# Attention, a layer of four experts and a squared MLP: the fourth expert taken from seven block products to eight, and the sums of x from GpSimd to VectorE

## The chip, the cores and the metric

One core of one Trainium2 chip runs the whole program. The metric is device time in microseconds (us); before the change it is 771.84 us, the median of three runs (766.21 to 772.74). The profiled execution is a run of its own: 764.1 us.

## The reference

```python
def reference(q, k, v, s, domain_probs, moe_w1, moe_w2, w_in, w_out):
    x = attention(q, k, v, s)               # causal, with a bias from cumsum(max(s, 0)); 2 x 8 heads, 576 x 64
    x = x.transpose(0, 2, 1, 3).reshape(1152, 512)
    p = domain_probs / (domain_probs.sum(-1, keepdims=True) + 1e-9)
    out = 0
    for e in range(4):                      # w1[e] 512 x 1024, w2[e] 1024 x 512
        out += p[:, e:e + 1] * (np.maximum(x @ w1[e], 0) @ w2[e])
    r = np.maximum(out @ w_in, 0)           # w_in 512 x 2048
    return (r * r) @ w_out                  # w_out 2048 x 512
```

All of it is float32. The weights of the last MLP reach the chip as 64-bit numbers (two 32-bit words each) and are turned into float32 there ("decoded").

## The kernel before, in words

**Numbers.** Every operand of the expert layers and of the MLP is split in a high part h = round(x) and a low part l = x - h, and each product is three matmuls (h h, h l, l h). `split` pairs are a cast on ScalarE and a subtraction (`less`, L77) on VectorE or GpSimd.

**The stages.** Experts are counted 0 to 3 here as in the code, E = 4. (1) Attention, with expert 0 for the first 768 tokens filled into its gaps. (2) Expert 0 for the last 384 tokens (L1012), eight steps. (3) Experts 1 to 3 (L1035 to L1066): layer one is done by block products after Strassen and Winograd, seven products of 128 x n x 256 for what plainly takes eight. A group (L962) is one quarter pair q of an expert's weights (12 in all, `NQ`) with one block b of tokens (512 or 640), so there are 24 groups. It has 7 products of 6 matmuls (L934) and, from the group before, the units of layer two (L952). (4) The MLP, as two layers e = E and e = E + 1 of 1024 hidden columns, in 48 steps (L1086): a step is one 128-column slice f of layer one for 384 tokens (`l1_pe`, 12 matmuls of 384 columns, L201; `l1_evac`) and, two steps behind it, the matching part of layer two (`y_quantum`, 9 matmuls of 512 columns, L236). Each layer goes over three thirds of the tokens, eight f each.

**Evacuation.** `l1_evac` of an expert is a relu on ScalarE (L215) and max and subtract on VectorE (L216, reading PSUM). In the MLP it is relu r (L221), g = max(ph, 0) r on VectorE (L223, the last reader of the PSUM tile ph), the cast of g (L226) on ScalarE and h's low part on VectorE (L227, both inputs in SBUF). There are two ph tiles and three h tiles.

**Turning of x.** The output of the experts for 128 tokens is turned by four transposes (L271) into a ph tile and split into xh and xl (`x2_evac`). The nine turnings lie in the last units of the groups (four) and in MLP steps 1 to 5.

**Decoding** (`w_split_double`, L121). One piece is 128 x 512 weights of an MLP half; there are 16 pieces per half, 32 in all. In order: ScalarE L135, GpSimd L137, then VectorE L140, L143, L145, L146, L148, then the cast L154 and GpSimd's subtraction L77. The temporaries dy and dtop exist once; dval has `NV` = 5 buffers. It is a generator with three stages; `advance()` moves each piece in work by one stage, once per step (five times per group). The ten first pieces are put into the last four groups (L1043), six into steps 0 to 4, the 16 of the second half into steps 5 to 20. `slot_free` holds the last stage back until the step at which the slot of its weight is free. A step's y needs one piece of the second weight.

**Order of the work.** A scheduler orders each engine's instructions by a model of their times, with the program's order as priority; SP (which issues the loads) keeps the program's order. Each engine then runs its queue in order.

**Memory.** Weight slots are taken in a ring of nine (`w_slot`), three of the MLP's have their own (`wc_p`). `load_next` keeps three raw pieces ahead (tag raw_w, three buffers, experts and MLP alike); there are 80 loads. `val_tile` takes its tiles from the dval ring.

**Sums.** `x_sums` (L827) makes the sums of blocks of x. For each block b and k2 it adds high and low parts of four quarters on GpSimd (L836, 16 instructions in all), takes four differences on VectorE (L847 to L850) and splits four results; that of b12 is put in place of x's own quarter in xh and xl. `w_pair` (L866) makes the sums and splits of one weight quarter pair (L884 to L912).

Of the kernel before, what the change touches and what calls it, by code (L numbers as in the profile page):

```python
# [8 lines left out]
F32 = mybir.dt.float32  # L9
F32R = mybir.dt.float32r  # L10
# [6 lines left out]
P = 128  # L17
# [16 lines left out]

AK, AQ = slice(0, 2), slice(32, 34)
NA = 6
NV = 5

BLOCKS = ((0, 256), (512, 320))
HIGHEST = 1.4375 * 2.0**-96  # L40
# [3 lines left out]
def fused_kernel(ctx, tc, qk, v, s, dp, w1, w2, wi, wo, out):  # L44
# [40 lines left out]
    def w_load(e, kind, g, half):  # L85
        n = slice(half * 512, (half + 1) * 512)
        if e < E:
            raw = st_pools[0].tile([P, 512], F32, tag=st_pools[2], name="raw_w", bufs=st_pools[1])
            nc.sync.dma_start(out=raw, in_=(w1 if kind == 1 else w2)[e, g, :, n])
        else:  # L90
            raw = st_pools[0].tile([P, 1024], U32, tag="raw_w", name="raw_d", bufs=st_pools[1])
            nc.sync.dma_start(out=raw, in_=(wi if kind == 1 else wo)[e - E, g, half].bitcast(U32))
        wraw[e, kind, g, half] = raw

# [6 lines left out]

    def w_new(e, kind, g):
        if (e, kind, g) not in wt:
            if e == E + 1 and kind == 1 and g:
                wt[e, kind, g] = wc_p.tile([P, 2, 1024], F32R, tag="w", name="w")
            else:
                wt[e, kind, g] = w_slot()
        return wt[e, kind, g]
# [49 lines left out]

    def slot_free(e, kind, g):

        return (e, kind) != (E + 1, 2) or now[0] >= starts[e] - 8 + 2 * g + 2

    PIECES = [(k, g, half) for k in (1, 2) for g in range(4) for half in range(2)]

# [626 lines left out]

    pc_p = ctx.enter_context(tc.tile_pool(name="pc", bufs=1, space=PSUM))
    w8_p = ctx.enter_context(tc.tile_pool(name="w8", bufs=1))
    dbl_p = ctx.enter_context(tc.tile_pool(name="dbl", bufs=1))
    late_p = ctx.enter_context(tc.tile_pool(name="late", bufs=1))
    acc_b = late_p.tile([P, NTILE - NA, DM], F32, name="acc_b")
    for t in range(NA, NTILE):
# [1 line left out]
    st_pools[:] = [late_p, 3, "raw_w"]  # L799
    y_count[0] = 0  # L800
    SKEW = 2
    NQ = (E - 1) * 4


    loads = [(1 + q // 4, k, q % 4, half) for q in range(NQ) for k in (1, 2) for half in range(2)]
    loads += [(e, *piece) for e in (E, E + 1) for piece in PIECES]
    nload = [0]

    def load_next():
# [4 lines left out]
    for _ in range(3):  # L814
# [3 lines left out]
    str_p = sa.enter_context(tc.tile_pool(name="str", bufs=1))  # L818
    h_pools[:] = [str_p, 640, 4]
    tx = {  # L820
        (b, i): str_p.tile([P, 2, 2, n], F32R, name=f"tx{b}{i}") for b, (_, n) in enumerate(BLOCKS) for i in (1, 2, 4)
    }

    def val_tile():
        return dbl_p.tile([P, 512], F32, tag="dval", name="dval", bufs=NV)

    def x_sums(b, k2):  # L827

        t0, n = BLOCKS[b]

        def whole(kk, t):
            x = val_tile()[:, :n]
            nc.gpsimd.tensor_tensor(  # L836
                x, xh[:, kk, t : t + n].bitcast(F32), xl[:, kk, t : t + n].bitcast(F32), op=ALU.add
            )
            return x

        def split(x, hi, lo):
            nc.scalar.copy(hi, x)
            less(nc.vector, lo, x, hi)

        b12, b11 = whole(k2, t0 + n), whole(k2, t0)
        b22, b21 = whole(2 + k2, t0 + n), whole(2 + k2, t0)
        nc.vector.tensor_tensor(b11, b12, b11, op=ALU.subtract)  # L847
        nc.vector.tensor_tensor(b12, b22, b12, op=ALU.subtract)
        nc.vector.tensor_tensor(b22, b22, b11, op=ALU.subtract)
        nc.vector.tensor_tensor(b21, b21, b22, op=ALU.subtract)  # L850
        for i, x in ((1, b11), (2, b22), (4, b21)):
            split(x, tx[b, i][:, 0, k2, :], tx[b, i][:, 1, k2, :])
        split(b12, xh[:, k2, t0 + n : t0 + 2 * n], xl[:, k2, t0 + n : t0 + 2 * n])

    def x_part(b, name, half, k2):
        t0, n = BLOCKS[b]
        x = (xh, xl)[half]
        if name in ("b11", "b21"):
            return x[:, k2 + (2 if name == "b21" else 0), t0 : t0 + n]
        if name in ("b22", "t3"):  # L860
            return x[:, k2 + (2 if name == "b22" else 0), t0 + n : t0 + 2 * n]
        return tx[b, int(name[1])][:, half, k2, :]

    pw = {}
# [1 line left out]
    def w_pair(q):  # L866

        e, g = 1 + q // 4, q % 4

        def quarters(half):  # L870
            return wraw[e, 1, g, half].rearrange("p (k j n) -> p k j n", k=2, j=2)

        def two(x):
            return x.rearrange("p (k n) -> p k n", k=2)

        def raw_parts():
            pw[q] = [w_slot()]
            d = pw[q][0]
            left, right = quarters(0), quarters(1)
            a11, a21 = left[:, :, 0, :], left[:, :, 1, :]  # L880
            a12, a22 = right[:, :, 0, :], right[:, :, 1, :]
            s12, s34 = val_tile(), val_tile()
            s1, s2, s3, s4 = (two(x[:, i : i + 256]) for x in (s12, s34) for i in (0, 256))
            nc.vector.tensor_tensor(s1, a21, a22, op=ALU.add)  # L884
            nc.vector.tensor_tensor(s3, a11, a21, op=ALU.subtract)
            nc.vector.tensor_tensor(s2, s1, a11, op=ALU.subtract)
            nc.vector.tensor_tensor(s4, a12, s2, op=ALU.subtract)
            nc.scalar.copy(two(d[:, 0, 512:768]), a11)
            nc.vector.tensor_tensor(two(d[:, 1, 512:768]), a11, two(d[:, 0, 512:768].bitcast(F32)), op=ALU.subtract)
            raw = wraw[e, 1, g, 1]  # L890
            nc.scalar.copy(d[:, 0, :512], raw)
            less(nc.vector, d[:, 1, :512], raw, d[:, 0, :512])
            for half in range(2):
                wraw.pop((e, 1, g, half))
                load_next()
            pw[q].append((s12, s34))

        def sum_parts(i):
            if i == 0:
                pw[q].insert(1, w_slot())  # L900
            d, x = pw[q][1], pw[q][2][i]
            c = slice(i * 512, i * 512 + 512)
            nc.scalar.copy(d[:, 0, c], x)  # L903
            less(nc.gpsimd, d[:, 1, c], x, d[:, 0, c])

        def second(half):
            raw = wraw.pop((e, 2, g, half))
            t = w_new(e, 2, g)
            n = slice(half * 512, (half + 1) * 512)
            nc.scalar.copy(t[:, 0, n], raw)  # L910
            less(nc.gpsimd, t[:, 1, n], raw, t[:, 0, n])
            load_next()  # L912

        return [
            [raw_parts],
            [lambda: sum_parts(0), lambda: sum_parts(1), lambda: second(0), lambda: second(1)],
        ]

    W_AT = {"a12": (0, 0, 256), "a22": (0, 128, 256), "a11": (0, 512, 128)}
# [89 lines left out]

    c = (768, 384)  # L1010
    prep = {q: w_pair(q) for q in range(NQ)}
    for i in range(NF):  # L1012
        l1_evac(0, c, i, l1_pe(0, c, i))
        if i >= SKEW:
            y_quantum(0, c, i - SKEW)
        if i in (1, 2):
            x_sums(0, i - 1)
        if i >= 4:
            for op in prep[(i - 4) // 2][i % 2]:
                op()  # L1020
    units = [lambda f=f: y_quantum(0, c, f) for f in range(NF - SKEW, NF)]


# [13 lines left out]
    for q in range(2, NQ):  # L1037
        for part in range(2):
            side[2 * q - 3 + part] += prep[q][part]
    side[0] += [lambda: x_sums(1, 0)]  # L1040
    side[1] = [lambda: x_sums(1, 1)] + side[1]
    last = len(groups) - 1
    for g in range(4):  # L1043
        for half in range(2):
            side[last - 3 + g].append(lambda g=g, half=half: decode(E, 1, g, half))
    for half in range(2):
        side[last].append(lambda half=half: decode(E, 2, 0, half))
    x2q = []
    for i, (q, b) in enumerate(groups):
        todo = units  # L1050
        n_units, n_side = len(todo), len(side[i])
# [2 lines left out]
        def do_next(k):  # L1054
# [5 lines left out]
            while done[1] < n_side * (k + 1) // 5:  # L1060
                side[i][done[1]]()
                done[1] += 1
            advance()

        units = group(q, b, do_next)
    now[0] = -1  # L1066


    for t, unit in enumerate(units):
        if t < 4:  # L1070
            x2_evac(t, x2_pe(t))
        unit()
    sa.close()
    mlp_p = ctx.enter_context(tc.tile_pool(name="mlp", bufs=1))
    h_pools[:] = [mlp_p, 384, 3]
    wc_p = ctx.enter_context(tc.tile_pool(name="wc", bufs=3))
    y_slots[:] = [yb_p] * 5 + [pc_p]
    thirds = [(0, 384), (384, 384), (768, 384)]
    seq = [(e, c, f) for e in (E, E + 1) for c in thirds for f in range(NF)]
    starts = {E: 0, E + 1: 24}  # L1080
    wsched = {}
    for n, (g, half) in enumerate((g, half) for g in range(1, 4) for half in range(2)):
        wsched.setdefault(n * 5 // 6, []).append((E, 2, g, half))
    for n, piece in enumerate(PIECES):
        wsched.setdefault(5 + n, []).append((E + 1, *piece))
    for i in range(len(seq) + SKEW):  # L1086
        now[0] = i
        advance()
        if i < len(seq):
            e, c, f = seq[i]  # L1090
            l1_evac(e, c, f, l1_pe(e, c, f))
        if 1 <= i < 6:
            x2_evac(3 + i, x2_pe(3 + i))
        if SKEW <= i < len(seq) - HOLD + SKEW:
            y_quantum(*seq[i - SKEW])
        for w in wsched.get(i, []):
            decode(*w)

    e, c, _ = seq[-1]
    tiles = range(c[0] // P, (c[0] + c[1]) // P)  # L1100
# [54 lines left out]
```

## Time and profile before

| | |
|---|---|
| median of three runs | 771.84 us |
| the three runs | 771.84, 772.74, 766.21 us |
| the profiled execution | 764.1 us |
| its span, first to last instruction | 762.3 us |
| mean granted clock of TensorE | 0.991 |

In the rows below times are in us unless they say ns. PE is TensorE, PEld its weight loads, DVE VectorE, ACT ScalarE, POOL GpSimd, SP the engine that issues the DMAs. Matmuls overlap in the pipeline, so the sum of their records is more than the time they take; paces are therefore read from start to start. A bracket at the end of a row of the timeline is the idle time of the engine before it and what ended it.

### The profile page before, as it was taken

What the parts mean: (1) busy time and instruction counts of PE and PEld (TensorE: products, weight loads), DVE (VectorE), ACT (ScalarE), POOL (GpSimd) and SP (SyncE); (2) the same over time, 40 slices, a digit from 0 to 9 for tenths busy, and PEclk for the clock granted to TensorE, in tenths of its full rate; (3) what the DMA queues carried; (4) which work ended last, traced back from release to release, by engine and by line L of the source; (5) the groups of instructions that cost most, each with busy time, mean ns of one, the idle gap of its engine ahead of it and who ended that gap; (6) DMA issues with size and microseconds to landing.
All of it is one profiled execution on the core that took longest, in us unless ns stands there. A gap on an engine that the chain in (4) does not pass through costs nothing.

```text
span 762.3 us, 11177 instructions
## 1 busy us (share of the span) xinstructions
PE 714.1 (94%) x3974; PEld 609.4 (80%) x3974; DVE 472.1 (62%) x1061; ACT 322.3 (42%) x756; POOL 225.5 (30%) x256
## 2 busy tenths in 40 slices
PE   5989999989988999999999999999877999968998
PEld 3567778767977898989989999898766899857996
DVE  7886666553389446454464546777767786777332
ACT  4787666553244243342343424334433333333221
POOL 6654433331277022130221304221222212222000
PEclk9999999999999999999999999999999999999999
DMA  6752232200122012010120103211222221220111
GB/s 185 217 163 70 76 96 63 57 24 1 42 74 66 28 39 73 28 56 28 47 65 28 56 29 103 77 56 55 84 77 68 78 78 61 83 84 0 42 42 41
DMA packets 28823, 50.37 MB, mean 66 GB/s; under 512 B 3424, under 2 KB 12144, under 8 KB 28768
## 3 DMA queue, kind: packets, MB, share of 16 engines
q1 hardware_dynamic: 28768, 49.67, 21.3%
q8 instruction: 31, 0.51, 0.3%
q14 instruction: 24, 0.20, 0.1%
HBM read 45.28 MB, written 2.54 MB: 63 GB/s over the span
## 4 chain that ended last, share of the span: by engine, by line
PE 79%; DVE 10%; issue 3%; DMA 3%; ACT 3%; POOL 2%; SPq 0%; DVEq 0%; POOLq 0%; ACTq 0%
PE y L952 19%; PE ph L201 15%; PE y L236 14%; PE ph L934 12%; PE o L602 5%; PE pc L934 5%; PE pt L555 4%; PE s L464 2%; DVE h L227 2%; PE s L465 2%; POOL w L77 1%; DMA raw_w<-in_w 1%; PE s L449 1%; DVE dtop L143 1%; ACT dy L135 1%
## 5 line engine op out<-in xcount | busy, mean ns | idle before, releaser
L201 PE MATMUL ph<-xh,w 128*128 128x384 f32 (+1 forms) x640 | 168.2, 330 | 21.3 <-DVE g L223 17.8
L952 PE MATMUL y<-w,h 128*128 128x512 f32 x648 | 170.1, 393 | 0.0
L236 PE MATMUL y<-w,h 128*128 128x512 f32 x648 | 165.5, 396 | 4.3 <-ACT w L154 4.3
L236 PEld LDWEIGHTS y<-w,h 128*128 128x128 f32 x648 | 119.6, 189 | 29.1 <-ACT w L154 8.5
L201 PEld LDWEIGHTS ph<-xh,w 128*128 128x128 f32 x640 | 115.6, 192 | 32.5 <-DVE g L223 22.7
L77 POOL TENSOR_TENSOR w<-dval,w 128x512 fp32r<-128x512 f32 x56 | 76.8, 1375 | 188.5 <-ACT w L903 143.1
L952 PEld LDWEIGHTS y<-w,h 128*128 128x128 f32 x648 | 114.9, 188 | 16.2
L201 PE MATMUL ph<-xl,w 128*128 128x384 f32 (+1 forms) x320 | 104.3, 327 | 0.0
L934 PE MATMUL ph<-xh,w 128*128 128x256 f32 (+1 forms) x288 | 69.2, 297 | 3.4 <-DVE h L983 1.9
L221 ACT ACTIVATE r<-ph 128x384 f32<-128x384 f32 x48 | 23.6, 491 | 108.6 <-PE ph L201 103.7
L201 PEld LDWEIGHTS ph<-xl,w 128*128 128x128 f32 x320 | 61.5, 192 | 3.5 <-issue 1.5
L532 POOL TENSOR_SCALAR p<-p,stat 128x128 f32<-128x128 f32 (+8 forms) x80 | 45.7, 585 | 52.7 <-DVE stat L529 35.4
L227 DVE TENSOR_TENSOR h<-g,h 128x384 fp32r<-128x384 f32 x48 | 40.2, 838 | 31.6 <-ACT h L226 31.6
L137 POOL TENSOR_SCALAR dy<-dy 128x512 f32<-128x512 f32 x32 | 20.3, 635 | 130.0 <-ACT dy L135 130.0
L982 ACT ACTIVATE h<-c 128x256 fp32r<-128x256 f32 (+1 forms) x72 | 31.9, 444 | 57.4 <-DVE c L979 57.4
L934 PEld LDWEIGHTS ph<-xh,w 128*128 128x128 f32 x288 | 50.1, 188 | 7.2 <-DVE h L983 2.3
L516 ACT ACTIVATE p<-p,stat 128x128 f32<-128x128 f32 (+9 forms) x80 | 46.6, 583 | 21.0 <-DVE stat L502 19.3
L983 DVE SCALAR_TENSOR_TENSOR h<-c,h 128x256 fp32r<-128x256 f32 (+1 forms) x72 | 39.7, 551 | 20.1 <-ACT h L982 19.9
L223 DVE SCALAR_TENSOR_TENSOR g<-ph,r 128x384 f32<-128x384 f32 x48 | 26.7, 556 | 36.4 <-ACT r L221 35.8
L934 PE MATMUL ph<-tx,w 128*128 128x256 f32 (+1 forms) x288 | 45.9, 296 | 0.3 <-ACT p L973 0.3
L934 PEld LDWEIGHTS ph<-tx,w 128*128 128x128 f32 x288 | 42.6, 189 | 3.3 <-ACT p L973 0.5
L502 DVE CUSTOM_DVE_ANT_0 p<-s,mask 128x448 f32<-128x448 f32 (+7 forms) x64 | 30.5, 477 | 22.7 <-PE pt L555 10.9
(120 smaller groups left out, 1137.3 us busy)
## 6 DMA issues: line engine op xcount, KB each, us to landing
raw_w<-in_w SPq DMA_DIRECT2D x64, 256.0 KB
raw_d<-in_wi SPq DMA_DIRECT2D x16, 512.0 KB
raw_d<-in_wo SPq DMA_DIRECT2D x16, 512.0 KB
raw<-in_qk SPq DMA_DIRECT2D x40, 144.0 KB
v<-in_v SPq DMA_DIRECT2D x8, 256.0 KB
out<-acc_a SPq DMA_DIRECT2D x6, 256.0 KB
tl<-th SPq DMA_DIRECT2D x8, 144.0 KB
raw_p<-in_qk SPq DMA_DIRECT2D x4, 256.0 KB
```

Source lines behind the costliest of these rows:

```text
L77: eng.tensor_tensor(out_, a, b.bitcast(F32), op=ALU.subtract)
L201: nc.tensor.matmul(ps[:, :n], lhsT=w1_ap(e, wh, kk, f), rhs=x[:, kk, t0 : t0 + n], start=(i == 0), stop=(i == 3 * KD - 1),)
L227: nc.vector.tensor_tensor(t[:, 1, :n], g[:, :n], t[:, 0, :n].bitcast(F32), op=ALU.subtract)
L236: mm = nc.tensor.matmul(ps, lhsT=h[:, hh, o : o + P], rhs=w2_ap(e, wh, f), start=(f == 0 and i == 0), stop=(f == NF - 1 and i == 2),)
L502: nc.vector.tensor_tensor_reduce(t.p[: t.n, a:z], ps[: t.n, : z - a], t.bias[:, a:z], scale=-0.125, scalar=init, op0=ALU.add, op1=ALU.min, ...
L516: nc.scalar.activation(t.p[: t.n, : t.w], t.p[: t.n, : t.w], AF.Exp, bias=t.nmax, scale=-1.0, accum_out=t.st[: t.n, 4 + t.c : 5 + t.c],)
L532: nc.gpsimd.tensor_scalar(t.p[: t.n, : t.w], t.p[: t.n, : t.w], t.st[: t.n, 6 + t.c : 7 + t.c], 1.0, op0=ALU.mult, op1=ALU.mult)
L602: nc.tensor.matmul(u.o[i * D : (i + 1) * D, qs - u.q0 : u.nq], lhsT=vv[:kn, j, i * D : (i + 1) * D], rhs=rhs, start=(j == 0), stop=(j == j ...
L934: nc.tensor.matmul(ps[:, :n], lhsT=pw[q][s][:, wh, c : c + P], rhs=x_part(b, xn, xx, k2), start=(first and m == 0), stop=(m == 5), skip_gr ...
L952: nc.tensor.matmul(ps, lhsT=hs[j][:, hh, o : o + P], rhs=wt[e, 2, g][:, wh, j * DM : (j + 1) * DM], start=(g % 2 == 0 and i == 0 and j == ...
L982: nc.scalar.activation(hs[j][:, 0, cols], ps[:, :n], AF.Relu)
L983: nc.vector.scalar_tensor_tensor(hs[j][:, 1, cols], ps[:, :n], 0.0, hs[j][:, 0, cols].bitcast(F32), op0=ALU.max, op1=ALU.subtract)
```

## The change

Expert 3 goes from the groups to the front of the plain steps: `NQ` is 8 (experts 1 and 2), there are 16 groups, and `seq` has 72 steps, 24 each for e = 3, E and E + 1. The splits of expert 3's weights lie in the last four groups and in steps 0 to 3. The 16 decoded pieces of E lie at steps 3 to 21, those of E + 1 at steps 23 to 43. The turnings of x follow each third of expert 3 (one per step, from the step after its last y). `NV` is 6, dbl_p opens after the groups, raw_d has three buffers of its own there, the value tiles of the sums are four of their own ("val"), and other weights use wc_p. The sums of `x_sums` are on VectorE, and b12 has a tile of its own (expert 3 needs x as it is). `w_pair` does the same instructions in smaller parts (sums, raw_hi, raw_lo, sum_hi, sum_lo, second_hi, second_lo). The preparations of the first groups are placed by the list `first`.

```diff
-NV = 5
+NV = 6
...
-            raw = st_pools[0].tile([P, 1024], U32, tag="raw_w", name="raw_d", bufs=st_pools[1])
+            raw = dbl_p.tile([P, 1024], U32, tag="raw_d", name="raw_d", bufs=3)
...
-            if e == E + 1 and kind == 1 and g:
+            if g and (e, kind) in ((E, 1), (E + 1, 2)):
...
-        return (e, kind) != (E + 1, 2) or now[0] >= starts[e] - 8 + 2 * g + 2
+        return kind == 1 or now[0] >= starts[e] - 8 + 2 * g + 2
...
-    NQ = (E - 1) * 4
+    PLAIN = E - 1
+    NQ = (PLAIN - 1) * 4
...
-    loads += [(e, *piece) for e in (E, E + 1) for piece in PIECES]
+    loads += [(e, *piece) for e in range(PLAIN, E + 2) for piece in PIECES]
...
-        return dbl_p.tile([P, 512], F32, tag="dval", name="dval", bufs=NV)
+        return str_p.tile([P, 512], F32, tag="val", name="val", bufs=4)
...
-            nc.gpsimd.tensor_tensor(
+            nc.vector.tensor_tensor(
                 x, xh[:, kk, t : t + n].bitcast(F32), xl[:, kk, t : t + n].bitcast(F32), op=ALU.add
             )
...
-        for i, x in ((1, b11), (2, b22), (4, b21)):
+        for i, x in ((1, b11), (3, b12), (2, b22), (4, b21)):
             split(x, tx[b, i][:, 0, k2, :], tx[b, i][:, 1, k2, :])
-        split(b12, xh[:, k2, t0 + n : t0 + 2 * n], xl[:, k2, t0 + n : t0 + 2 * n])
...
+    first = [[lambda: x_sums(0, 0)], [lambda: x_sums(0, 1)], [], []]
+    first += [prep[0][0], prep[0][1], prep[1][0], prep[1][1][:2]]
...
-        if i in (1, 2):
-            x_sums(0, i - 1)
-        if i >= 4:
-            for op in prep[(i - 4) // 2][i % 2]:
-                op()
+        for op in first[i]:
+            op()
...
-    side[0] += [lambda: x_sums(1, 0)]
+    side[0] = prep[1][1][2:] + [lambda: x_sums(1, 0)]
...
-            side[last - 3 + g].append(lambda g=g, half=half: decode(E, 1, g, half))
-    for half in range(2):
-        side[last].append(lambda half=half: decode(E, 2, 0, half))
+            side[last - 3 + g].append(lambda g=g, half=half: split(PLAIN, 1, g, half))
+    for g in range(2):
+        for half in range(2):
+            side[last].append(lambda g=g, half=half: split(PLAIN, 2, g, half))
...
-    for t, unit in enumerate(units):
-        if t < 4:
-            x2_evac(t, x2_pe(t))
+    for unit in units:
         unit()
     sa.close()
...
+    dbl_p = ctx.enter_context(tc.tile_pool(name="dbl", bufs=1))
...
-    seq = [(e, c, f) for e in (E, E + 1) for c in thirds for f in range(NF)]
-    starts = {E: 0, E + 1: 24}
-    wsched = {}
-    for n, (g, half) in enumerate((g, half) for g in range(1, 4) for half in range(2)):
-        wsched.setdefault(n * 5 // 6, []).append((E, 2, g, half))
-    for n, piece in enumerate(PIECES):
-        wsched.setdefault(5 + n, []).append((E + 1, *piece))
+    seq = [(e, c, f) for e in range(PLAIN, E + 2) for c in thirds for f in range(NF)]
+    starts = {e: 24 * (e - PLAIN) for e in range(PLAIN, E + 2)}
+    wsched = {n: [(PLAIN, 2, 2 + n // 2, n % 2)] for n in range(4)}
+    for e in (E, E + 1):
+        for n, piece in enumerate(PIECES):
+            at = starts[e - 1] + (3 + n * 5 // 4 if e == E else n * 22 // 16 - 1)
+            wsched.setdefault(at, []).append((e, *piece))
+    x2q = []
...
-        if 1 <= i < 6:
-            x2_evac(3 + i, x2_pe(3 + i))
-        if SKEW <= i < len(seq) - HOLD + SKEW:
-            y_quantum(*seq[i - SKEW])
+        if x2q and x2q[0][0] <= i:
+            t = x2q.pop(0)[1]
+            x2_evac(t, x2_pe(t))
+        if i >= SKEW:
+            e, c, f = seq[i - SKEW]
+            if i - SKEW < len(seq) - HOLD:
+                y_quantum(e, c, f)
+            if e == E - 1 and f == NF - 1:
+                x2q += [(i + 1 + n, t) for n, t in enumerate(range(c[0] // P, (c[0] + c[1]) // P))]
         for w in wsched.get(i, []):
-            decode(*w)
+            split(*w) if w[0] < E else decode(*w)
```

## Rows read from the trace of the kernel before

**Rows 1.** The page: busy time of each engine, share of the span, instructions.

```profile
PE 714.1 (94%) x3974; PEld 609.4 (80%) x3974; DVE 472.1 (62%) x1061; ACT 322.3 (42%) x756; POOL 225.5 (30%) x256
```

**Rows 2.** Busy time by stretch: length, then each engine's, clock, DMA share, GB/s.

```profile
200.00:235.00 35.00, 32.66 (x161) 29.64 (x160) 28.09 (x45) 14.42 (x34) 24.43 (x22) 0.95 0.23 76
235.00:262.00 27.00, 23.35 (x143) 20.34 (x143) 17.73 (x36) 9.81 (x25) 8.41 (x7) 1.00 0.16 49
...
379.80:426.90 47.10, 47.10 (x277) 42.60 (x277) 24.52 (x50) 17.28 (x40) 10.85 (x8) 1.00 0.15 45
...
527.60:587.20 59.60, 47.41 (x233) 40.43 (x232) 43.04 (x70) 22.63 (x44) 16.78 (x18) 0.97 0.24 77
587.20:650.00 62.80, 62.80 (x318) 57.02 (x317) 48.58 (x82) 24.59 (x48) 15.21 (x17) 1.00 0.22 69
650.00:699.00 49.00, 39.11 (x188) 32.57 (x187) 36.21 (x56) 16.45 (x33) 14.67 (x16) 1.00 0.19 63
```

**Rows 3.** The chain of waits in order of time: start, length, what.

```profile
385.64 2.73 PE y L952 x12
...
432.72 2.73 PE y L952 x12
...
527.85 2.10 PE ph L201 x12
...
603.14 2.04 PE y L236 x9
...
648.53 2.04 PE y L236 x9
...
663.70 1.42 DVE h L227
...
690.17 1.42 DVE h L227
...
752.38 6.13 PE y L236 x27
```

**Rows 4.** Timeline of PE in the last stage: start, length, instructions, idle before.

```profile
522.64 0.60 PE L271 MATMUL ph<-ident,acc_a 128*128 128x128 f32 x4
...
533.50 0.45 PE L201 MATMUL ph<-xh,w 128*128 128x384 f32 x1 [1.05 <-DVE g L223]
...
669.92 0.98 PE L236 MATMUL y<-w,h 128*128 128x512 f32 x3 [0.45 <-ACT w L154]
672.37 0.45 PE L201 MATMUL ph<-xh,w 128*128 128x384 f32 x1 [1.47 <-DVE g L223]
```

**Rows 5.** Timeline of VectorE: ends of decoded pieces, and one piece whole.

```profile
490.88 0.68 DVE L148 SCALAR_TENSOR_TENSOR dval<-dtop,dy 128x512 f32<-128x512 f32 x1
...
507.45 0.69 DVE L148 SCALAR_TENSOR_TENSOR dval<-dtop,dy 128x512 f32<-128x512 f32 x1
...
641.38 0.68 DVE L148 SCALAR_TENSOR_TENSOR dval<-dtop,dy 128x512 f32<-128x512 f32 x1
...
648.21 0.69 DVE L148 SCALAR_TENSOR_TENSOR dval<-dtop,dy 128x512 f32<-128x512 f32 x1
...
672.23 0.42 DVE L140 TENSOR_SCALAR dtop<-dy 128x512 uint32<-128x512 uint32 x1
...
674.60 0.69 DVE L148 SCALAR_TENSOR_TENSOR dval<-dtop,dy 128x512 f32<-128x512 f32 x1
```

**Rows 6.** Groups over the span: busy us, mean ns of one, idle before and releasers.

```profile
L201 PE MATMUL ph<-xh,w 128*128 128x384 f32 x448 | 126.4, 345 | 20.1 <-DVE g L223 17.8 <-DVE h L216 2.3
...
L77 POOL TENSOR_TENSOR w<-dval,w 128x512 fp32r<-128x512 f32 x56 | 76.8, 1375 | 188.5 <-ACT w L903 143.1 <-ACT w L154 42.0 <-PE y L952 3.3
...
L227 DVE TENSOR_TENSOR h<-g,h 128x384 fp32r<-128x384 f32 x48 | 40.2, 838 | 31.6 <-ACT h L226 31.6
```

**Rows 7.** The same groups, VectorE alone, from 200 to 262 us.

```profile
L216 DVE SCALAR_TENSOR_TENSOR h<-ph,h 128x384 fp32r<-128x384 f32 x8 | 4.4, 546 | 0.0
...
L847 DVE TENSOR_TENSOR dval<-dval 128x320 f32<-128x320 f32 x2 | 1.0, 478 | 0.0
```

More of the change, by code (lines that the diff above doesn't have):

```diff
@@ L793, in fused_kernel @@
     w8_p = ctx.enter_context(tc.tile_pool(name="w8", bufs=1))
-    dbl_p = ctx.enter_context(tc.tile_pool(name="dbl", bufs=1))
     late_p = ctx.enter_context(tc.tile_pool(name="late", bufs=1))
@@ L820, in fused_kernel @@
     tx = {
-        (b, i): str_p.tile([P, 2, 2, n], F32R, name=f"tx{b}{i}") for b, (_, n) in enumerate(BLOCKS) for i in (1, 2, 4)
+        (b, i): str_p.tile([P, 2, 2, n], F32R, name=f"tx{b}{i}") for b, (_, n) in enumerate(BLOCKS) for i in (1, 2, 3, 4)
     }
     def val_tile():
-        return dbl_p.tile([P, 512], F32, tag="dval", name="dval", bufs=NV)
+        return str_p.tile([P, 512], F32, tag="val", name="val", bufs=4)
     def x_sums(b, k2):
@@ L859, in x_part @@
             return x[:, k2 + (2 if name == "b21" else 0), t0 : t0 + n]
-        if name in ("b22", "t3"):
-            return x[:, k2 + (2 if name == "b22" else 0), t0 + n : t0 + 2 * n]
+        if name == "b22":
+            return x[:, k2 + 2, t0 + n : t0 + 2 * n]
         return tx[b, int(name[1])][:, half, k2, :]
@@ L874, in two, with parts, sums @@
             return x.rearrange("p (k n) -> p k n", k=2)
-        def raw_parts():
-            pw[q] = [w_slot()]
-            d = pw[q][0]
+        def parts():
             left, right = quarters(0), quarters(1)
[L880 to L883, printed above, removed]
+            return left[:, :, 0, :], left[:, :, 1, :], right[:, :, 0, :], right[:, :, 1, :]
+        def sums():
+            a11, a21, a12, a22 = parts()
+            x = [val_tile(), val_tile()]
+            s1, s2, s3, s4 = (two(v[:, i : i + 256]) for v in x for i in (0, 256))
             nc.vector.tensor_tensor(s1, a21, a22, op=ALU.add)
@@ L887, in raw_parts, with raw_hi, raw_lo @@
             nc.vector.tensor_tensor(s4, a12, s2, op=ALU.subtract)
[L888 to L892, printed above, removed]
+            pw[q] = [w_slot(), w_slot(), x]
+        def raw_hi():
+            d = pw[q][0]
+            nc.scalar.copy(two(d[:, 0, 512:768]), parts()[0])
+            nc.scalar.copy(d[:, 0, :512], wraw[e, 1, g, 1])
+        def raw_lo():
+            d = pw[q][0]
+            nc.vector.tensor_tensor(
+                two(d[:, 1, 512:768]), parts()[0], two(d[:, 0, 512:768].bitcast(F32)), op=ALU.subtract
+            )
+            less(nc.vector, d[:, 1, :512], wraw[e, 1, g, 1], d[:, 0, :512])
             for half in range(2):
@@ L895, in raw_parts, with sum_hi, sum_lo, second_hi @@
                 load_next()
[L896 to L901, printed above, removed]
-            c = slice(i * 512, i * 512 + 512)
[L903 to L908, printed above, removed]
+        def sum_hi():
+            for i, x in enumerate(pw[q][2]):
+                nc.scalar.copy(pw[q][1][:, 0, i * 512 : i * 512 + 512], x)
+        def sum_lo(i):
+            c = slice(i * 512, i * 512 + 512)
+            less(nc.gpsimd, pw[q][1][:, 1, c], pw[q][2][i], pw[q][1][:, 0, c])
+        def second_hi(half):
+            nc.scalar.copy(w_new(e, 2, g)[:, 0, half * 512 : half * 512 + 512], wraw[e, 2, g, half])
+        def second_lo(half):
             n = slice(half * 512, (half + 1) * 512)
-            nc.scalar.copy(t[:, 0, n], raw)
-            less(nc.gpsimd, t[:, 1, n], raw, t[:, 0, n])
+            t = wt[e, 2, g]
+            less(nc.gpsimd, t[:, 1, n], wraw.pop((e, 2, g, half)), t[:, 0, n])
             load_next()
         return [
-            [raw_parts],
-            [lambda: sum_parts(0), lambda: sum_parts(1), lambda: second(0), lambda: second(1)],
+            [sums, raw_hi, raw_lo],
+            [
+                sum_hi,
+                lambda: (sum_lo(0), second_hi(0)),
+                lambda: (sum_lo(1), second_hi(1)),
+                lambda: (second_lo(0), second_lo(1)),
+            ],
         ]
@@ L1039, in fused_kernel, with split @@
             side[2 * q - 3 + part] += prep[q][part]
-    side[0] += [lambda: x_sums(1, 0)]
+    side[0] = prep[1][1][2:] + [lambda: x_sums(1, 0)]
     side[1] = [lambda: x_sums(1, 1)] + side[1]
     last = len(groups) - 1
+    def split(*piece):
+        w_split(*piece)
+        load_next()
     for g in range(4):
         for half in range(2):
-            side[last - 3 + g].append(lambda g=g, half=half: decode(E, 1, g, half))
-    for half in range(2):
-        side[last].append(lambda half=half: decode(E, 2, 0, half))
-    x2q = []
+            side[last - 3 + g].append(lambda g=g, half=half: split(PLAIN, 1, g, half))
+    for g in range(2):
+        for half in range(2):
+            side[last].append(lambda g=g, half=half: split(PLAIN, 2, g, half))
     for i, (q, b) in enumerate(groups):
@@ L1062, in do_next @@
                 done[1] += 1
-            advance()
         units = group(q, b, do_next)
-    now[0] = -1
-    for t, unit in enumerate(units):
-        if t < 4:
-            x2_evac(t, x2_pe(t))
+    for unit in units:
         unit()
```

## The prediction

> **What bounds the kernel now.** I read the page's engine line first: PE is busy 94% of the span, which says little, because it is a mean over stages [rows 1]. The busy time by stretch comes next. The reader is to see that in four product groups (379.8 to 426.9) and in 587.2 to 650 PE has no idle time at all, while 527.6 to 587.2 leaves 59.60 - 47.41 = 12.2 us idle, 650 to 699 leaves 9.9 us, and the start of the expert stage 2.3 and 3.7 us [rows 2]. The chain of waits gives the pace. Two places four groups apart lie 432.72 - 385.64 = 47.08 us from each other, so a group is 11.77 us. A step of a plain layer (12 matmuls of layer one, 9 of layer two) takes (648.53 - 603.14) / 11 = 4.126 us where PE never waits. In 663.70 to 690.17 the chain runs through VectorE's L227 instead, four steps in 26.47 us, 6.62 us each [rows 3]. PE's own timeline says what a 6.62 us step waits for: 0.45 us on ScalarE's cast of the second weight (L154), which the decoding has only just delivered, and 1.47 us on VectorE's L223, which frees the PSUM tile [rows 4]. So in both stretches the weights of the last MLP arrive one piece per step, exactly as they are consumed. The whole last stage lasts 752.38 + 6.13 - 527.85 = 230.7 us [rows 3]; 48 steps at 4.126 are 198.1 us, and five turnings of x (L271) at 0.60 us or less are 3.0 us [rows 4]. **29.6 us of it are waits for decoded weights** and what follows from them.
>
> Why are they late? One piece is about 3.06 us of VectorE (L140 at 672.23 to the end of L148 at 675.29), behind a step on ScalarE and one on GpSimd, and its buffer dy is single, so pieces follow each other. L148 comes every (507.45 - 490.88) / 2 = 8.28 us among the product groups and every 6.83 us beside the squared layer at full PE speed [rows 5]. Thirty-two pieces begin in the last four groups, and the last is wanted about 200 us later. At 6.8 to 8.3 us each that is not enough.
>
> **The change part by part.**
>
> *Expert three in eight products.* Eight groups go, 2 x 47.08 = 94.2 us. Twenty-four plain steps come, 24 x 4.126 = 99.0 us. Cost: +4.9 us of PE. I take the step at 4.126 although its evacuation differs: L216 instead of r, g, cast and L227. That is less for VectorE (0.546 us in one instruction against L227 with 0.84 us and L223 besides) and hidden under PE [rows 6, 7]. The sums of this expert's weights, its sum splits and the additions L979 go too. They lay under fully busy PE, with VectorE at 24.5 of 47.1 us [rows 2], so I cost them at nothing.
>
> *Decoding beside expert three.* The first piece starts at about step 4 of 72, where before it lay among the groups, and the last is due at step 57. Sixteen pieces are spread at one per 1.25 steps (5.2 us) beside expert three, sixteen at one per 1.375 steps beside the first half of the MLP. VectorE's load beside expert three is 0.546 + 3.06 / 1.25 = 3.0 us of a 4.126 us step (without its evacuation of y, three instructions in eight steps). Beside the MLP it was busy 48.58 of 62.80 us, which are 15.2 steps, with nine pieces; at one per 1.375 steps it would have eleven, 48.58 + 2 x 3.06 = 54.7 [rows 2, 5, 7]. It fits, but not loosely. What pace will the chain of one dy keep? The bounds are 5.2 us (the schedule) and 8.28 us (among groups). I take 6.0 us beside expert three, since there a step has one short VectorE instruction where the groups have several that wait for PE, and 6.83 us beside the MLP, the row of the same work. From step 4 (447 us by the sum below) E's pieces are then done at 447 + 96 = 543, and its last is due at step 33 (568). The last MLP half is done at 543 + 109 = 652 and due at step 57 (667). Both are in time, so the 29.6 us go. What is late next is the turning of x: nine, each between a layer one product and its y, where before gaps of 1.05 us on L223 stood behind it [rows 4]. Now each has nine y matmuls beside it, so I take half of 1.05 us for nine, and 1 us for the change of stage: **6 us remain**, bounds 0 and 12.
>
> *New waits.* The ScalarE cast of a second weight waits until its slot is free (program step 18 + 2g, 42 + 2g). Behind it on ScalarE stand the relu of the next step and the next piece's L135. The slot's last reader is layer one of step 17 + 2g (41 + 2g), which has run by then, so it costs nothing in order; if it slips, six value buffers (five before) cover it, and a missed one costs one 4.1 us step. On SP the eighty loads keep their order. The raw tiles of the MLP now lie in memory that opens when the groups end, so their first load goes out around step 1; the first weight is due at step 24, 83 us later. The splits of expert three's weights in the last four groups take no more than the preparation that stood there. All that is zero; if the cover of the last group fails, a single late split costs about 1 us.
>
> *Sums of x.* Sixteen instructions leave GpSimd and come to VectorE. The nearest VectorE row of kind and width (L847, 320 columns; half of them are narrower) is 0.478 us, so some 16 x 0.48 = 7.7 us are added in a stretch where VectorE is busy 28.1 of 35 and 17.7 of 27 us [rows 2, 7]. Of PE's 2.3 + 3.7 = 6.0 us idle there 2.3 wait for VectorE's L216 [rows 2, 6]. Bounds: -6 us, all of it, and +4 us, half of the added work, if L216 falls further behind. I take -2, the gap on L216, because GpSimd's slower turn no longer stands ahead of the subtractions. The product of b12 now has its own tile; that is the same number of splits, so nothing.
>
> The Trainium skill has a rule that speaks against this move ("SBUF — State Buffer", section "SBUF: two separate sides"): a VectorE operation with two SBUF inputs and a GpSimd operation reading SBUF exclude each other for the whole instruction. The trace agrees in kind: L227, both inputs in SBUF, takes 0.84 us in the mean and 1.42 us in the chain, L216, with one input in PSUM, 0.546 [rows 3, 6, 7]. By the rule each of the sixteen sums could stand behind one GpSimd subtraction (1.375 us [rows 6]), an estimate of 22 us against 16.2 us of VectorE's idle time there, which would put about +6 us in place of -2; the same rule also frees the others from sixteen GpSimd instructions, and I keep the -2.
>
> **Sum.** The last stage starts at 527.85 - 94.2 - 4 x 0.60 (four turnings lay there) - 2 = 429.3. Then 72 x 4.126 = 297.1, nine turnings 5.4, waits 6, and from PE's end to the span's end 762.3 - 758.5 = 3.8: span 741.6 us. The profiled execution is 764.1 for a span of 762.3, so 743.4 in its terms, 20.7 us less. It lies 7.7 us under the median of the three runs (771.84, 772.74, 766.21); carried over whole, that gives 751.1, and by the lowest run 745.5. I say **748 us**.
>
> **Rivals.**
> 1. *The decoding stays late (slower).* The pace remains 8.28 us, as in the groups, because VectorE's queue sets decoding steps behind evacuations that wait for PE. Then 447 + 32 x 8.28 = 712, 45 us after step 57: 748 + 45 = 793 us. It eats the whole gain from (667 + 21 - 447) / 32 = 7.5 us per piece on. For it: the groups' rows and the single dy. Against: 6.83 us beside the heavier layer [rows 5]. Chance 0.10.
> 2. *Weights are in time, but decoding ahead of the evacuation in VectorE's queue makes PE wait for its PSUM tile.* At 0.8 us for each of 32 pieces that is 26 us, 774: no change. For it: the 1.05 us gap on L223. Against: 587.2 to 650, with nine pieces and no idle PE [rows 2, 4, 5]. Chance 0.13.
> 3. *No waits at all remain*, and the start loses none: 748 - 6 - 4 = 738 us. Chance 0.12.
>
> The forecast has 0.65. Its own range is 739 to 760 (residual waits 0 to 12, start -6 to +4, run to run from 745.5 to 751.1). The 8-in-10 range is 736 to 768, which leaves out rival 1 and most of rival 2. About 1% is what a measurement tells here, 764.1 to 779.6: faster 0.77 (forecast and rival 3), same 0.13, slower 0.10.
>
> **What would show it.** Right: PE idle under 8 us from the end of the groups to the end; steps at about 4.13 us across 72; no y matmul waiting for L154; L148 every 5 to 6.5 us beside expert three; sixteen groups still 11.77 us each. Wrong: 6.6 us steps again, in the MLP's first or second half (rival 1); gaps on L216 or L223 after decoding instructions (rival 2); a start of the expert stage with more than 6 us idle (the sums of x).

## The result and the profile after

The changed kernel takes 735.8 us in the median of four runs (734.63 to 741.11), beside it the kernel before 769.44 us (766.21 to 772.74): a ratio of 0.958, 95% interval 0.951 to 0.964. The forecast was 748 us, with 739 to 760 as its own range and 736 to 768 as the wide one: the result lies at the lower edge of the wide range and under the narrow one. Thirteen later runs of the kernel before have 766.7 us in the median, so the gain is nearer 31 us than 34.

The profiled execution is the slowest of the four, 741.11 us with a span of 739.3. Attention, whose code is the same, lasted until 207.3 us in it (granted clock 0.93 up to there), and until 200.2 us in the profile before (0.98) and 200.8 us in a later run of nearly the same kernel; these 7 us are not the change's. Places are therefore compared from the start of the expert stage, its first matmul of 384 columns. From there to the end of the span it takes 562.1 us before and 532.0 us now: 30.1 us less.

The busy time by stretch of the changed kernel (columns as in rows 2) answers to [rows 2]:

```profile
207.46:242.00 34.54, 34.54 (x184) 31.77 (x184) 27.14 (x60) 15.58 (x35) 11.52 (x8) 1.00 0.26 84
242.00:269.00 27.00, 25.13 (x149) 21.63 (x148) 20.51 (x42) 10.41 (x26) 5.56 (x4) 1.00 0.11 39
...
431.30:540.00 108.70, 108.12 (x559) 98.19 (x558) 73.32 (x117) 33.10 (x63) 24.97 (x27) 1.00 0.25 79
540.00:640.00 100.00, 100.00 (x516) 91.42 (x515) 72.09 (x125) 39.11 (x77) 24.96 (x26) 1.00 0.21 69
640.00:735.56 95.56, 95.56 (x484) 86.66 (x482) 48.40 (x82) 28.49 (x56) 10.96 (x11) 1.00 0.10 36
```

The reader is to see the first two columns: PE's busy time is the whole stretch nearly everywhere. The plain steps have 0.58 us of idle PE in 304 us, where 12.2 + 9.9 us stood in two stretches before. The start of the expert stage keeps 1.9 of 6.0 us.

The chain of waits in order of time answers to [rows 3]:

```profile
280.65 2.75 PE y L961 x12
...
327.78 2.75 PE y L961 x12
...
576.75 2.04 PE y L236 x9
...
630.40 2.04 PE y L236 x9
...
729.44 6.13 PE y L236 x27
```

Four groups take 47.13 us, as before. Thirteen steps take 630.40 - 576.75 = 53.65 us, 4.127 each, with a decoding of the last MLP half beside them. No step of 6.6 us is left. The last wait of PE in the start of the stage and its only one after that, 0.58 us at the seam of the groups and the steps, are in its timeline:

```profile
254.53 0.98 PE L943 MATMUL pc<-tx,w 128*128 128x256 f32 x6 [1.17 <-DVE c L988]
...
438.08 1.66 PE L236 MATMUL y<-w,h 128*128 128x512 f32 x6 [0.58 <-ACT h L215]
```

The decoding itself did not become faster. VectorE's timeline, the first and the last piece of each half, answers to [rows 5]:

```profile
445.21 0.69 DVE L148 SCALAR_TENSOR_TENSOR dval<-dtop,dy 128x512 f32<-128x512 f32 x1
...
553.28 0.69 DVE L148 SCALAR_TENSOR_TENSOR dval<-dtop,dy 128x512 f32<-128x512 f32 x1
...
561.58 0.69 DVE L148 SCALAR_TENSOR_TENSOR dval<-dtop,dy 128x512 f32<-128x512 f32 x1
...
674.71 0.69 DVE L148 SCALAR_TENSOR_TENSOR dval<-dtop,dy 128x512 f32<-128x512 f32 x1
```

Fifteen intervals make 7.20 us a piece for the MLP's first half and 7.54 us for its second: slower than the forecast's 6.0 and 6.83. It is in time all the same, because it begins earlier. The first and the last piece in VectorE's timeline of the kernel before:

```profile
471.21 1.75 DVE L148 SCALAR_TENSOR_TENSOR dval<-dtop,dy 128x512 f32<-128x512 f32 x1
...
701.42 0.69 DVE L148 SCALAR_TENSOR_TENSOR dval<-dtop,dy 128x512 f32<-128x512 f32 x1
```

Over all 31 intervals the pace is 7.43 us before and 7.40 us now. Counted from the start of the expert stage, the first piece moves from 271.0 to 237.9 us and the last from 501.2 to 467.4 us, while the MLP begins where it did (327.5 and 325.5 us). So it is the earlier start that the change buys, not a faster decoding beside a lighter evacuation.

### The profile page after: what moved, and what is told of

Its sections match the earlier page's. It is cut to its first block, busy times and chain, and to the rows that moved or that the text cites. A ratio compares the mean times of both kernels' runs of the same rounds, so it can differ in the third digit from the quotient of the medians.

```text
span 739.3 us, 10968 instructions
## 1 busy us (share of the span) xinstructions
PE 711.9 (96%) x3926; PEld 614.3 (83%) x3926; DVE 448.7 (61%) x1028; ACT 309.4 (42%) x716; POOL 188.4 (25%) x224
## 4 chain that ended last, share of the span: by engine, by line
PE 89%; DVE 5%; DMA 3%; POOL 1%; issue 1%; ACT 1%; SPq 0%; POOLq 0%; DVEq 0%; ACTq 0%
PE ph L201 27%; PE y L236 25%; PE y L961 13%; PE ph L943 8%; PE o L602 5%; PE pt L555 3%; PE pc L943 3%; PE s L464 2%; DMA raw_w<-in_w 2%; PE s L465 2%; POOL w L77 1%; DVE w L77 1%; DMA s<-in_s 1%; PE ph L271 1%; DVE tx L77 0%
## 5 line engine op out<-in xcount | busy, mean ns | idle before, releaser
L201 PE MATMUL ph<-xh,w 128*128 128x384 f32 (+1 forms) x832 | 218.2, 328 | 1.6 <-DVE h L216 1.6
L201 PEld LDWEIGHTS ph<-xh,w 128*128 128x128 f32 x832 | 149.5, 190 | 8.1 <-DVE h L216 2.4
L201 PE MATMUL ph<-xl,w 128*128 128x384 f32 (+1 forms) x416 | 135.7, 327 | 0.0
L201 PEld LDWEIGHTS ph<-xl,w 128*128 128x128 f32 x416 | 78.9, 190 | 5.0 <-issue 1.5
L137 POOL TENSOR_SCALAR dy<-dy 128x512 f32<-128x512 f32 x32 | 20.3, 634 | 198.4 <-ACT dy L135 132.9
L223 DVE SCALAR_TENSOR_TENSOR g<-ph,r 128x384 f32<-128x384 f32 x48 | 26.7, 556 | 50.1 <-ACT r L221 50.1
L77 POOL TENSOR_TENSOR w<-val,w 128x512 fp32r<-128x512 f32 x16 | 23.3, 1461 | 130.0 <-ACT w L903 89.2
L215 ACT ACTIVATE h<-ph 128x384 fp32r<-128x384 f32 (+1 forms) x56 | 24.5, 444 | 69.2 <-PE ph L201 59.1
L77 POOL TENSOR_TENSOR w<-dval,w 128x512 fp32r<-128x512 f32 x32 | 41.7, 1302 | 37.1 <-ACT w L154 37.1
L216 DVE SCALAR_TENSOR_TENSOR h<-ph,h 128x384 fp32r<-128x384 f32 (+1 forms) x56 | 27.5, 495 | 38.8 <-ACT h L215 38.7
L943 PE MATMUL ph<-tx,w 128*128 128x320 f32 (+1 forms) x288 | 45.8, 296 | 0.7 <-ACT u L982 0.7
L555 PE MATMUL pt<-ident,p 128*128 128x128 f32 (+3 forms) x232 | 40.6, 289 | 4.0 <-POOL p L532 3.7
```

Source lines behind the costliest of these rows:

```text
L77: eng.tensor_tensor(out_, a, b.bitcast(F32), op=ALU.subtract)
L201: nc.tensor.matmul(ps[:, :n], lhsT=w1_ap(e, wh, kk, f), rhs=x[:, kk, t0 : t0 + n], start=(i == 0), stop=(i == 3 * KD - 1),)
L216: nc.vector.scalar_tensor_tensor(t[:, 1, :n], ps[:, :n], 0.0, t[:, 0, :n].bitcast(F32), op0=ALU.max, op1=ALU.subtract)
L555: nc.tensor.transpose(tp_ap(t, j), t.p[: t.n, kt[j] : kt[j + 1]], ident[: t.n, : t.n])
L943: nc.tensor.matmul(ps[:, :n], lhsT=pw[q][s][:, wh, c : c + P], rhs=x_part(b, xn, xx, k2), start=(first and m == 0), stop=(m == 5), skip_gr ...
```

## The experiments

The theory was that the gain is time for a decoding whose pace one dy buffer sets, and that the sums of x on VectorE give a little at the start. Against it stood: that queue order sets the pace, that the plain steps' lighter evacuation is the gain, and that the placement of the preparation cleared the start.

**One part alone: two buffers of dy in the kernel before.**

```diff
-NV = 5
+NV = 4
-        y = tmp(F32, "dy")
+        y = tmp(F32, "dy", 2)
```

> The kernel before with two buffers of dy (dval 4 instead of 5, for the room), nothing else. If the single dy sets the pace of the decoding: L148 comes every 6 us or less among the product groups instead of 8.28, the waits of 29.6 us in the last stage fall by 15 to 25 us, ratio 0.97 to 0.98. If the order of VectorE's and ScalarE's queues (decoding steps behind evacuations) sets it: the pace stays at 7 to 8 us, ratio 0.995 to 1.01.

Measured: 750.32 us (749.49 to 751.17), ratio 0.977, interval 0.973 to 0.981. The second and the last piece in VectorE's timeline of this run:

```profile
482.42 0.68 DVE L148 SCALAR_TENSOR_TENSOR dval<-dtop,dy 128x512 f32<-128x512 f32 x1
...
647.14 0.69 DVE L148 SCALAR_TENSOR_TENSOR dval<-dtop,dy 128x512 f32<-128x512 f32 x1
```

Thirty intervals are 164.7 us, 5.49 us each, where the kernel before has 7.43 us. The single dy set the pace, and about half of the gain (766.8 us, the median of seven runs of the kernel before beside it, to 750.3) is to be had by that alone. But the kernel does not reach 736, although its PE work is the smaller: VectorE is now the limit. Its slices on the page (busy tenths, 40 slices) stand at 9 from the 27th to the 34th:

```profile
DVE  6785666454178656455464455899999999823232
```

The chain of waits of this run goes through the decoding itself, of which this is one piece:

```profile
602.38 1.59 DVE dtop L143
```

**One part alone: the sums of x on VectorE in the kernel before.**

```diff
-            nc.gpsimd.tensor_tensor(
+            nc.vector.tensor_tensor(
                 x, xh[:, kk, t : t + n].bitcast(F32), ...
```

> The kernel before with the sixteen sums of x on VectorE, nothing else. If GpSimd's sums make the PE gaps at the start of the expert stage (6.0 us): 3 to 6 us less, ratio 0.992 to 0.996, and PE idle there under 3 us. If the new placement and the smaller parts of the preparation are what took them away: ratio 1.00, the gaps stay.

Measured: 760.26 us, ratio 0.990, interval 0.986 to 0.994, a little faster than either theory said. The gaps at the start became smaller and others took their place: PE is idle 4.1 us there, not under 3. The largest gap left in PE's timeline:

```profile
244.53 0.39 PE L934 MATMUL ph<-xh,w 128*128 128x256 f32 x1 [2.00 <-DVE c L979]
```

The first y L952 x12 after 270 us is the same place in the groups in every run. By the chain of the kernel before it comes 79.1 us after the start of the expert stage (200.2):

```profile
279.29 2.72 PE y L952 x12
```

In this run it comes 75.8 us after (202.9):

```profile
278.75 2.72 PE y L952 x12
```

So the start is 3.3 us shorter, but not by the sums alone: the granted clock was 0.95 over 35 us of it before [rows 2], a mean of full level (2.4 GHz) and half, and 1.00 here: an estimated 1.7 us (35 x 0.05). A further 2.7 us lie in the last stage, whose waiting steps take 6.1 us here; why this edit shortens them stays open. The next run asks the same question more cleanly.

**One part undone: the sums back on GpSimd in the changed kernel.**

```diff
-            nc.vector.tensor_tensor(
+            nc.gpsimd.tensor_tensor(
                 x, xh[:, kk, t : t + n].bitcast(F32), ...
```

> The changed kernel with the sixteen sums of x back on GpSimd, nothing else. If the engine of the sums makes the gaps at the start of the expert stage: 3 to 6 us more, 739 to 742. If their placement does: 736, no change.

Measured: 739.44 us (738.66 to 741.69), 3.6 us over the changed kernel's median. The gap on L216 is back in PE's timeline:

```profile
238.18 0.39 PE L943 MATMUL ph<-xh,w 128*128 128x256 f32 x1 [1.39 <-DVE h L216]
```

The same place comes 76.8 us after the stage's start, 73.4 us in the changed kernel and 74.1 to 74.3 us in two later runs with the same start. So the engine is worth some 3 us. That the other 2.3 us (79.1 to 76.8) come from the placement in smaller parts is not shown. The first run leaves sums and placement as they were (only the ring that the sums share is one buffer shorter), and there the place comes 76.6 us after the start (202.3):

```profile
278.94 2.72 PE y L952 x12
```

One profile each cannot tell 2.3 us of placement from a difference of that size without it.

**A later decoding, by the schedule's numbers.**

```diff
-            at = starts[e - 1] + (3 + n * 5 // 4 if e == E else n * 22 // 16 - 1)
+            at = starts[e - 1] + (11 + n * 13 // 16 if e == E else n * 22 // 16 - 1)
```

> The changed kernel with the 16 pieces of E put at steps 11 to 23 instead of 3 to 21, nothing else. If the gain is the earlier start of the decoding, at a pace of 7.2 to 7.5 us a piece that stays as it is: all ends some 8 steps (33 us) later, steps of 6.6 us with waits on L154 come back, 20 to 30 us more, 756 to 766. If the place of the decoding beside expert three's lighter evacuation is the gain and the start is not: under 5 us more.

Measured: 736.33 us (735.51 to 737.95), no change. Both theories expected something here and the edit did not make it: the first and the last piece come 238.8 and 466.6 us after the stage's start, 237.9 and 467.4 us in the changed kernel. VectorE's timeline of this run:

```profile
439.61 0.69 DVE L148 SCALAR_TENSOR_TENSOR dval<-dtop,dy 128x512 f32<-128x512 f32 x1
...
667.37 0.68 DVE L148 SCALAR_TENSOR_TENSOR dval<-dtop,dy 128x512 f32<-128x512 f32 x1
```

The step number did not place the pieces. The first one waited for its load here, as it did in the changed kernel (2.71 us there); ScalarE's timeline of this run:

```profile
435.47 0.66 ACT L135 ACTIVATE dy<-raw_d 128x512 f32<-128x512 f32 x1 [2.67 <-DMA raw_d<-in_wi]
```

That buffers and slots place the later ones is likely, but was not tested. So this run says nothing on the start of the decoding; the next one had to move it in another way.

**Less time for the decoding: half of expert three back to seven products.** Twenty groups, then 60 steps; the schedule of the pieces is shortened to fit.

```diff
-    NQ = (PLAIN - 1) * 4
+    NQ = (PLAIN - 1) * 4 + 2
...
-    seq = [(e, c, f) for e in range(PLAIN, E + 2) for c in thirds for f in range(NF)]
-    starts = {e: 24 * (e - PLAIN) for e in range(PLAIN, E + 2)}
+    seq = [(e, c, f) for e in range(PLAIN, E + 2) for c in thirds for f in range(4 if e == PLAIN else 0, NF)]
+    starts = {PLAIN: 0, E: 12, E + 1: 36}
```

> The changed kernel, but the first half of expert three's hidden columns goes back to seven products: 20 groups, then 60 steps (12 of expert three). PE work falls by half of 4.9 us. If the time that the decoding has decides: it begins some 47 us later, at 7.3 us a piece the 32nd comes about 725 where it is wanted about 677, so waits on L154 come back, 755 to 780. If decoding beside plain steps is enough whatever their number: 733 to 737.

Measured: 772.29 us (ten runs, 767.25 to 773.9), ratio 1.004, interval 1.001 to 1.007: the whole gain is gone with 12 steps of time for the decoding, although PE's work is smaller. The pace stays (487.59 to 711.47 for 31 intervals, 7.2 us), the first piece comes 284.8 us after the stage's start instead of 237.9, and PE waits again for the second weights, in both halves of the MLP, as its timeline shows:

```profile
569.77 0.96 PE L237 MATMUL y<-w,h 128*128 128x512 f32 x3 [1.68 <-ACT w L154]
575.86 0.98 PE L237 MATMUL y<-w,h 128*128 128x512 f32 x3 [1.68 <-ACT w L154]
...
690.82 1.65 PE L237 MATMUL y<-w,h 128*128 128x512 f32 x3 [2.47 <-ACT w L154]
```

In the stretches with these waits (columns as in rows 2) the granted clock is also below the full level, 0.97 and 0.89 in the mean, an estimated 6.8 us (63 x 0.03 + 45 x 0.11) besides PE's idle time:

```profile
527.00:590.00 63.00, 48.21 (x234) 41.26 (x233) 50.51 (x75) 23.40 (x45) 18.17 (x20) 0.97 0.25 77
...
660.00:705.00 45.00, 35.40 (x145) 28.61 (x144) 30.69 (x48) 13.18 (x26) 11.17 (x12) 0.89 0.19 59
```

The other theory, that decoding beside plain steps is enough whatever their number, is out.

**The same half, with two buffers of dy** (the edit of the first run, with six value buffers).

> The same half kernel with two buffers of dy. If the single dy sets the pace and 5.7 us a piece is then to be had, as in the first run: 492 + 32 x 5.7 = 674, just in time, 733 to 742. If VectorE is full by then and PE waits for its evacuations: 742 to 755.

Measured: 756.74 us (755.48 to 757.47), ratio 0.985. The pace is 5.35 us (487.77 to 653.58, 31 intervals) and no wait on L154 is left, but PE waits for its evacuation. Two of the gaps in its timeline:

```profile
510.83 2.93 PE L237 MATMUL y<-w,h 128*128 128x512 f32 x6 [3.65 <-ACT h L215]
...
539.68 0.44 PE L201 MATMUL ph<-xh,w 128*128 128x384 f32 x1 [2.10 <-DVE g L223]
```

The weights are in time, so the first theory's 733 to 742 needed VectorE to bear it; it did not. The time is a little over the second theory's 742 to 755.

**The price of eight products: expert two plain as well.** Its successor's splits are spread over steps 10 to 26.

```diff
-    PLAIN = E - 1
+    PLAIN = E - 2
...
+    for n, piece in enumerate(PIECES):
+        at = (10, 11, 18, 19, 20, 21, 22, 23, 24, 24, 25, 25, 25, 25, 26, 26)[n]
+        wsched.setdefault(at, []).append((PLAIN + 1, *piece))
```

> The changed kernel with expert two in eight products as well (8 groups, 96 steps), nothing else. If a plain expert costs what the paces say, 99.0 against 94.2 us: 4.9 us more, 740 to 742. If its lighter side work gives something back: 736 to 738.

Measured: 742.26 us (740.74 to 743.58), 5.9 us over the run with the later schedule numbers (736.33) and 6.5 us over the changed kernel, with no idle PE in the steps but the 0.58 us at the seam. Counted from the start of the expert stage its profile takes 536.9 us, 4.9 more than the changed kernel's. The term of 4.9 us holds.

**A faster decoding where the weights are in time already: two buffers of dy and dtop in the changed kernel.**

```diff
-        y = tmp(F32, "dy")
+        y = tmp(F32, "dy", 2)
-        top, part = tmp(U32, "dtop"), y.bitcast(U32)
+        top, part = tmp(U32, "dtop", 2), y.bitcast(U32)
```

> The changed kernel with two buffers of dy and of dtop. The weights are in time already, so with either theory no gain: 735 to 737; the pieces come every 5 to 6 us instead of 7.3. If a faster decoding crowds VectorE against the evacuations: up to 745.

Measured: 747.53 us (746.43 to 749.73), some 11 us slower than the changed kernel and over the 745 expected. The busy time of the stretch in which it decodes:

```profile
428.70:590.00 161.30, 153.02 (x782) 137.12 (x781) 148.68 (x231) 60.16 (x113) 59.12 (x56) 1.00 0.33 105
```

And two of the gaps in PE's timeline there:

```profile
485.53 1.66 PE L236 MATMUL y<-w,h 128*128 128x512 f32 x6 [1.66 <-ACT h L215]
519.45 0.44 PE L201 MATMUL ph<-xh,w 128*128 128x384 f32 x1 [2.43 <-DVE h L216]
```

VectorE is busy 148.7 of 161.3 us, and PE is idle 8.3 us there. In the two gaps shown the evacuation stands behind decoding instructions (L216 on VectorE behind L148 and L145, L215 on ScalarE behind L135). The single buffer, which made the old kernel late, is not worth removing here.

## Why the prediction was right

**Right in its mechanism.** The 29.6 us of waits for decoded weights were real and were the gain: they went (0.58 us left), and they came back when the time for the decoding was cut (the half of expert three). In the trace 22.1 us of them are idle time of PE, and most of that ends on L223 (17.8 us [rows 6]), not on the weights; it went together with the waits on L154, and came back with them. That the single dy set the pace is shown by the first run. Expert three in eight products costs what the paces of groups and steps say. The account closes: 29.0 us of waits and 5.7 us at the start, less 4.9 us for the eight products, are 29.8 of the 30.1 us measured. Of the five signs named, four came; L148 every 5 to 6.5 us did not.

The sums on VectorE did not crowd it: the kernel was 3.6 us slower with them back on GpSimd. The rule of the Trainium skill that was weighed against it ("SBUF — State Buffer", section "SBUF: two separate sides") holds for single instructions: L143, with two inputs in SBUF, takes 0.69 us in the changed kernel, and 1.24 us in the mean of the 29 instances of the first run that overlap a GpSimd instruction. But the +6 us worked out by it did not come.

**Three terms were mis-sized.** The forecast span was 741.6 us; the measured one without the 7.1 us of the longer attention is 739.3 - 7.1 = 732.2, which is 9.4 us less.

- *The start: -2 taken, about -5.7 measured* (79.1 to 73.4 us from the stage's start to the same place). The gap on L216 went as reckoned; the step that failed is that the other gaps would stay: PE's idle time there fell from 6.0 to 1.9 us, by 4.1. The rest, some 1.7 us by estimate, is the granted clock, 0.95 in 200 to 235 us before [rows 2] and 1.00 after; the forecast had that row and no term for it. How much of it is the engine of the sums (some 3 us, by the run with that undone) and how much the placement stays open.
- *Waits that remain: 6 taken, 0.6 measured.* The forecast charged half a gap of 1.05 us to each of nine turnings of x, and 1 us to the change of stage. In the timeline of PE seven of the nine turnings now have y matmuls on both sides, the other two on one; the first:

```profile
473.31 1.75 PE L236 MATMUL y<-w,h 128*128 128x512 f32 x7
474.90 0.60 PE L271 MATMUL ph<-ident,acc_a 128*128 128x128 f32 x4
475.25 3.47 PE L236 MATMUL y<-w,h 128*128 128x512 f32 x14
```

  Those hide the evacuation whole, not by half: no turning is followed by idle time. The row of 1.05 us was from turnings with no y beside them, and was no fair measure.
- *The pace: 6.0 and 6.83 us taken, 7.20 and 7.54 measured.* This erred the other way and cost nothing, but by luck: two more terms were off as well. At the measured 7.40 us the forecast's own sum gives 447 + 32 x 7.40 = 684 us, 17 us after the due time of 667, and by rival 1 most of the gain gone. In the trace, less the 7.1 us, the first piece began at 434 us instead of 447 and the last was decoded at 668 instead of 652, a little after that due time. And the order on PE had more slack than the forecast counted: it ran slices of layer one ahead and did three steps' worth of y (27 matmuls) in one stretch after the last weight was cast. The last cast in ScalarE's timeline:

```profile
675.43 0.62 ACT L154 CAST w<-dval 128x512 fp32r<-128x512 f32 x1 [1.12 <-DVE dval L148]
```

The y matmuls behind it in PE's timeline:

```profile
677.04 1.52 PE L236 MATMUL y<-w,h 128*128 128x512 f32 x6
679.80 6.29 PE L236 MATMUL y<-w,h 128*128 128x512 f32 x27
```

**The rivals.** What happened is nearest to rival 3 (no waits remain, and the start loses none; 738 us, chance 0.12): both of its conditions held but for 0.6 us of waits and 1.9 us of idle time at the start. Rival 1 (the decoding stays late) is not what happened, but it is a true danger: with 12 steps fewer the time is that of the kernel before. Rival 2 (PE waits because decoding stands ahead of the evacuation) is shown as a mechanism by the runs with two buffers of dy, and only there. That nothing of this kind appears in the changed kernel goes together with its slower pieces, 7.2 us apart; that this alone is the reason was not isolated further.

**Carried over to the median,** the forecast took the middle between 745.5 and 751.1, because the profile before lay 7.7 us under the median of its three runs. The profile after lies 5.3 us over its own, and thirteen later runs put the median before at 766.7, 2.6 us over the profile. The offset of one execution does not carry over; that error is about as large as those of the terms.

**What stays open.** No kernel here beats the changed one. Seven products for all experts with a faster decoding (the first run) is held back by VectorE; a decoding with fewer VectorE instructions was not tried.

## What to carry to other kernels

Where an engine-bound stage waits for data that a side chain prepares, price the chain's pace against the time it has before the first use and the last, and look for work without such a need to put in front of it: here 4.9 us more on PE bought back 30. Speeding the chain itself is another way, but a poorer one where it shares an engine with the evacuation: it gave 16 us to the kernel whose weights were late (half of the gain), and took 11 us from the one whose weights were in time. And with a scheduler that orders the queues by a model of times, a step number need not place work: here eight steps more moved nothing, and the first piece waited for its load.

## What the runs showed of the hardware

VectorE's decoding instructions stretch beside GpSimd's subtraction, even one with a single input: in the changed kernel L140 takes 0.42 us in the 20 instances that overlap no GpSimd instruction, and 1.51 us where it starts just after GpSimd's. VectorE's timeline:

```profile
454.94 1.51 DVE L140 TENSOR_SCALAR dtop<-dy 128x512 uint32<-128x512 uint32 x1 [0.69 <-POOL dy L137]
```

And GpSimd's, at the same time:

```profile
454.87 1.29 POOL L77 TENSOR_TENSOR w<-dval,w 128x512 fp32r<-128x512 f32 x1
```

L216, which reads PSUM, keeps 0.556 us in the mean over all its 384-column instances; seven of them overlap a GpSimd instruction beside the decoding and take no longer. So a faster decoding does not only fill VectorE, its instructions grow: L143 takes 1.184 us in the mean in the first run, where 29 of 32 overlap a GpSimd instruction (L77, L137 or both; the other three take 0.68 us), and 0.688 us in the changed kernel, where none does. The groups over the span, in the first run:

```profile
L143 DVE SCALAR_TENSOR_TENSOR dtop<-raw_d,dtop 128x512 uint32<-128x512 uint32 x32 | 37.9, 1184 | 0.8
```

And in the changed kernel:

```profile
L143 DVE SCALAR_TENSOR_TENSOR dtop<-raw_d,dtop 128x512 uint32<-128x512 uint32 x32 | 22.0, 688 | 0.7
...
L216 DVE SCALAR_TENSOR_TENSOR h<-ph,h 128x384 fp32r<-128x384 f32 x32 | 17.7, 556 | 24.8 <-ACT h L215 24.8
```
